# Second-layer evictions given out behind each product, high parts read first, and the PSUM pools swapped

## The chip, the cores and the metric

The kernel runs on one core of one Trainium2 chip. The metric is the device time of one execution in microseconds (us), as the median of several runs. Beside the runs there is one profiled execution, whose trace gives every duration below.

## The reference

First a banded attention (4 batches, 8 heads, 768 positions, 64 wide), whose output becomes the 3072 x 512 matrix `x`. Then a mixture of 8 experts, weighted by a Sinkhorn iteration over the gate's logits:

```python
logits = x @ w_gate
P = np.exp(logits - logits.max())
for _ in range(8):
    P /= P.sum(1, keepdims=True) + 1e-09
    P /= P.sum(0, keepdims=True) + 1e-09
    P *= N / E
for e in range(E):
    h = np.maximum(x @ w1[e], 0.0)
    out += P[:, e:e + 1] * (h @ w2[e])
```

N is 3072, `w1` is 512 x 1024 and `w2` 1024 x 512 for each expert. All is float32.

## The kernel before

**Number form.** Every float32 operand is split into a high and a low part, and a product of two operands takes three TensorE matmuls (high x high, high x low, low x high). Block products go by a seven-product scheme, so each layer of a group is seven products m1 to m7 (first layer) and seven products p1 to p7 (second layer). Each product of one group takes six matmuls of 128x128 by 128x512 (first layer: two parts of the contraction; second layer: two banks of output). The code calls the time of six matmuls a slot (`SLOT = 1.36`).

**Tiling.** Tokens go in three passes. The hidden units of all experts are cut into 31 groups. Groups 0 to 3 are done while attention ends, by another routine (`layer1_strassen` and `second`); its last instructions are the y matmuls, whose results VectorE scales by the gate and adds up, and the exchange of the gate's rows (`between`, that is `spill_rows`: copies to `pcol`, two transposes `pr_ps`, copies to `prow`, DMAs). Groups 4 to 29 of the first pass go in thirteen pairs, (4, 5) to (28, 29). Group 30 follows alone, with a transposed second layer (`turned`, tile `o_t`).

**Order within a pair of the first pass** (called gA and gB). It is written out by the program and kept on each engine (class `Ordered`):
1. first layer of gA: seven slots, m3, m2, m1, m6, m5, m4, m7, in banks c, d, a, b, c, d, a;
2. p6, p4 and p2 of the pair before, which are still owed, follow here ("second" with `behind`), six slots;
3. first layer of gB, seven slots, same banks;
4. p3, p7, p5, p1 of both groups, eight slots.

The last pair has instead an "end" stage with all seven products, fourteen slots, whose results are combined by additions on VectorE and GpSimd (`join`, table `JOIN`).

**First layer** (`layer1_held`). ScalarE copies bank c of m3 to t3 (shown as `early<-bank_c`). VectorE subtracts m2's bank from it, adds t3 and m1's bank to t4, adds that to b of m6, scales, and so on. Every operand of the second layer then gets its high part by a ScalarE cast (`p<-bank_c` is p3's high, `p<-bank_b` p7's, `p<-full` and `p<-bank_d` p5's and p1's) and its low part by a VectorE subtraction (`p<-bank_c,p` is p3's low). The parts of p6, p4 and p2 are given out one by one from a generator in the list `tails` (`x<-bank_c`, `x<-bank_a`, `x<-full` for a gA; `p` for a gB).

**Second layer** (`held_second`). Sums of the second layer live in SBUF. p3, p7, p6 and p4 (`SEEDED`) begin from banks that ScalarE fills with the sum so far (`seed`, shown as `c_acc<-early`), and are emptied by ScalarE copies (`early<-c_acc`). The others are added by VectorE. Each product has two banks. The eviction of a product is noted in `filled_banks`, and given out at the start of the next product or behind the next m3.

**Weights.** In the first pass they are also made, by the generator `maker`: raw weights come by DMA, GpSimd makes sums, ScalarE casts the highs (`w<-raw`, `w<-ext`), GpSimd subtracts the lows (`w<-raw,w`), and the parts are stored in DRAM for passes two and three. A count of slots paces it (`clock`, `LEAD`).

**PSUM.** Pool `mps` has four banks (tag h), the first layer's. Pool `cps` has four banks (tag c), the second layer's; it opens where the y matmuls' pools (`yps`, `sps`) were.

## Time and profile before

| what | value |
|---|---|
| median of 3 runs | 2115.75 us (2113.81 to 2117.53) |
| the profiled execution's own time | 2113.67 us |
| span of its trace | 2111.7 us |
| granted TensorE clock, mean | 0.998 |
| TensorE busy | 2064.1 us, 98% |
| VectorE busy | 1441.8 us, 68% |
| ScalarE busy | 843.7 us, 40% |
| GpSimd busy | 1554.4 us, 74% |

PE is TensorE's matmuls, DVE is VectorE, ACT ScalarE, POOL GpSimd, SP SyncE with its DMA queue. Matmuls are pipelined, so two that follow each other start closer together than one lasts: six matmuls last 1.52 us and start 1.36 us after the six before. A busy share is a mean over stages with different limits; what one stage can give is read in that stage.

### The profile page before, as it was taken

Reading aid. Unit: us, or ns where it says so; the run is one execution under the profiler, and the core shown is the slowest. Engines: PE = TensorE matmul, PEld = TensorE weight load, DVE = VectorE, ACT = ScalarE, POOL = GpSimd, SP = SyncE. Lnnn points to the kernel's source line nnn. Section 1 sums busy time; section 2 is a strip of 40 time slices with the busy share of each in tenths; the row PEclk is TensorE's granted clock in tenths of the full one; section 3 lists DMA queues with packets and bytes.
Section 4 is the critical chain, followed back from the end, with each engine's and each line's share of the span. In section 5 each row is a group of like instructions: output and inputs, shape, how many; then the busy total and the mean of one; then the engine's idle time right before and its main releaser. Section 6 shows DMA issues by size and latency. Waiting matters only on the chain.

```text
span 2111.7 us, 30417 instructions
## 1 busy us (share of the span) xinstructions
PE 2064.1 (98%) x10365; PEld 1705.6 (81%) x10365; DVE 1441.8 (68%) x2539; ACT 843.7 (40%) x1772; POOL 1554.4 (74%) x1392
## 2 busy tenths in 40 slices
PE   8999998999999999999999999999999999999998
PEld 6888887777777777778888888888888888888887
DVE  8777787778888888955665566556746665566556
ACT  7777632565665655323222222222132222222221
POOL 6787886777777777757767767677677767767676
PEclk9999999999999999999999999999999999999999
DMA  6777576777767767795555565555956565566553
GB/s 155 206 219 212 171 261 243 265 259 269 268 252 291 259 255 278 289 350 205 203 201 199 193 210 204 198 204 186 387 207 205 193 211 200 183 209 215 189 205 137
DMA packets 229156, 477.48 MB, mean 226 GB/s; under 512 B 107072, under 2 KB 152576, under 8 KB 205696
## 3 DMA queue, kind: packets, MB, share of 16 engines
q1 hardware_dynamic: 228704, 474.40, 65.4%
q8 instruction: 84, 1.38, 0.3%
q0 software_dynamic: 288, 1.05, 0.1%
q14 instruction: 80, 0.66, 0.1%
HBM read 328.75 MB, written 146.64 MB: 225 GB/s over the span
## 4 chain that ended last, share of the span: by engine, by line
PE 74%; DVE 11%; ACT 5%; POOL 5%; issue 3%; DMA 1%; SPq 0%; ACTq 0%; DVEq 0%; POOLq 0%
PE c_acc L126 31%; PE bank_c L126 9%; PE bank_a L126 9%; PE bank_d L126 9%; PE bank_b L126 5%; PE o_t L126 2%; DVE early L70 2%; ACT p L70 2%; DVE full L70 2%; DVE x L70 1%; DVE p L70 1%; DVE bank_b L70 1%; DVE bank_c L70 1%; ACT w L70 1%; PE o_ps L126 1%
## 5 line engine op out<-in xcount | busy, mean ns | idle before, releaser
L126 PE MATMUL c_acc<-p,w 128*128 128x512 f32 x2838 | 682.4, 391 | 20.4 <-ACT early L70 12.0
L126 PEld LDWEIGHTS c_acc<-p,w 128*128 128x128 f32 x2838 | 529.8, 188 | 145.1 <-ACT early L70 22.4
L1635 DVE TENSOR_TENSOR early<-early,c_acc 128x512 f32<-128x512 f32 x308 | 210.8, 688 | 180.5 <-PE c_acc L126 180.5
L70 POOL TENSOR_TENSOR early<-raw,full 128x512 f32<-128x512 f32 x56 | 72.8, 1299 | 287.4 <-DVE raw L793 287.4
L126 PE MATMUL bank_c<-x,w 128*128 128x512 f32 x1068 | 272.4, 391 | 3.2 <-DVE p L70 3.2
L126 PE MATMUL bank_a<-m,w 128*128 128x512 f32 x1068 | 271.5, 389 | 2.0 <-DVE x L70 1.3
L126 PE MATMUL bank_d<-x,w 128*128 128x512 f32 x1068 | 271.5, 389 | 0.0
L70 POOL TENSOR_TENSOR w<-raw,w 128x512 fp32r<-128x512 f32 (+2 forms) x107 | 184.2, 1722 | 108.5 <-ACT w L70 108.5
L796 ACT CAST p<-raw 128x512 fp32r<-128x512 f32 x150 | 93.3, 622 | 417.9 <-DVE raw L793 328.9
L126 PEld LDWEIGHTS bank_c<-x,w 128*128 128x128 f32 x1068 | 201.1, 188 | 45.4 <-DVE p L70 3.6
L126 PEld LDWEIGHTS bank_a<-m,w 128*128 128x128 f32 x1068 | 200.3, 188 | 44.6 <-DVE x L70 1.8
L126 PEld LDWEIGHTS bank_d<-x,w 128*128 128x128 f32 x1068 | 200.7, 188 | 42.1 <-DMA x<-op_m 0.3
L70 POOL TENSOR_TENSOR p<-raw,p 128x512 fp32r<-128x512 f32 x152 | 196.8, 1295 | 3.7 <-ACT p L796 3.4
L126 PE MATMUL c_acc<-x,w 128*128 128x512 f32 x774 | 196.4, 389 | 0.0
L126 PEld LDWEIGHTS c_acc<-x,w 128*128 128x128 f32 x774 | 145.3, 188 | 30.2
L70 POOL TENSOR_TENSOR p<-full,p 128x512 fp32r<-128x512 f32 x120 | 156.2, 1302 | 3.7 <-ACT p L796 3.7
L804 DVE TENSOR_TENSOR early<-early,bank_d 128x512 f32<-128x512 f32 x63 | 43.3, 688 | 149.5 <-PE bank_d L126 147.1
L796 ACT CAST p<-full 128x512 fp32r<-128x512 f32 x121 | 75.4, 623 | 160.7 <-POOL full L70 140.2
L126 PE MATMUL bank_b<-m,w 128*128 128x512 f32 x534 | 135.5, 389 | 0.0
L126 PEld LDWEIGHTS bank_b<-m,w 128*128 128x128 f32 x534 | 100.2, 188 | 20.8
L371 ACT ACTIVATE p_sb<-p_sb,mx 128x256 f32<-128x256 f32 (+1 forms) x188 | 90.9, 488 | 22.6 <-DVE mx L366 22.1
L802 ACT COPY early<-bank_c 128x512 f32<-128x512 f32 x63 | 37.2, 590 | 150.9 <-PE bank_c L126 150.7
(385 smaller groups left out, 3857.5 us busy)
## 6 DMA issues: line engine op xcount, KB each, us to landing
w<-ws SPq DMA_DIRECT2D x124, 1024.0 KB, 4.9
w<-ws SPq DMA_DIRECT2D x122, 768.0 KB, 4.3
ws<-w SPq DMA_DIRECT2D x54, 1024.0 KB, 4.7
ws<-w SPq DMA_DIRECT2D x53, 768.0 KB, 5.7
raw<-in_moe_w_dram SPq DMA_DIRECT2D x54, 512.0 KB, 4.3
x<-p_rows SPq DMA_DIRECT2D x21, 512.0 KB, 4.9
x<-op_m SPq DMA_DIRECT2D x16, 512.0 KB, 10.5
ws<-w SPq DMA_DIRECT2D x4, 1792.0 KB, 8.5
```

Of the source, the lines that this page charges most:

```text
L70: return lambda *args, **kw: self.tc.keep_in_program_order(op(*args, **kw))
L126: return self.tc.keep_in_program_order(self.engine.matmul(*args, **kw))
L371: scalar.activation(out=views[u], in_=views[u], func=AF.Exp, bias=mx[:, u:u + 1], scale=-1.0, accum_out=sm[:, i, j:j + 1])
L796: engine.copy(out=ops[k][:, 0], in_=src)
L802: nc.scalar.copy(out=t3, in_=c)
L804: tt(out=t3, in0=t3, in1=d, op=ALU.subtract)
L1635: nc.vector.tensor_tensor(out=sums[k][q], in0=sums[k][q], in1=bank, op=ALU.add)
```

## The change

- The eviction of a second-layer product is given out directly behind its own last matmul instead of at the start of the next product or behind m3. The low of p6, p4 or p2 that is still owed follows the eviction.
- The three matmuls of a product now read weight low x operand high, then high x high, then weight high x operand low.
- From the second group on, the first layer works in `cps` and the second layer (`second_banks`) in `mps`; the first group (4) stays in `mps`. Passes two and three and `turned` are swapped likewise.
- `prow` and `pcol` move from a pool to `scratch`, a tile "gap" takes their place in the pool, the rows' exchange comes two y products later, and two of the y products use `mps`.
- In the "end" stage p3 and p7 are seeded, so that they are emptied by ScalarE copies; before, all seven were added by VectorE.
- The making of weights: at the start it runs on until block (5, 0, 0), the first high casts are not tied to the program's order, the gate's share is loaded first, the y spills go on the ordered queue; the last group has leads of its own.

```diff
+LAST_LEAD = {(0, 0): 20, (0, 1): 19, (1, 0): 13}
...
-                    y_ps = moe.layer2(t, wts[g], hs[i], yps, "y")
+                    y_ps = moe.layer2(t, wts[g], hs[i], *((mps, "h") if between and i * WT + t in (3, 4) else (yps, "y")))
...
-                    if between and (i, t) == (0, 1):
+                    if between and (i, t) == (0, 3):
                         between()
...
-                prow = hpool.tile([P, 3, P], F32, name="prow")
-                pcol = hpool.tile([P, E, NB, 2, WT], F32, name="pcol")
+                hpool.tile([P, WIDE], F32, name="gap")
+                prow = scratch[:, 2 * WIDE:2 * WIDE + 3 * P].rearrange("p (n c) -> p n c", n=3)
+                pcol = scratch[:, 3 * WIDE:3 * WIDE + E * NB * 2 * WT].rearrange("p (e b i t) -> p e b i t", e=E, b=NB, i=2)
...
+        def second_banks():
+            return [mps.tile([P, WIDE], F32, name="c_acc", tag="h") for _ in range(2)]
...
-                while clock[0] < used_at[b] - LEAD[layer, part][g % 2] and not hurry[0]:
+                while clock[0] < used_at[b] - (LEAD[layer, part][g % 2] if g < NG - 1 else LAST_LEAD[layer, part]) and not hurry[0]:
...
-                    act(out=high, in_=src)
+                    (act if clock[0] else nc.scalar.copy)(out=high, in_=src)
...
-                return moe.layer1_held(ops, lambda i: block(g, 0, i), share, (full[0], full[3], full[4]), ops_of[g], tmp, mps, "h", done)
-
-            return moe.layer1_scaled(ops, lambda i: blocks_of[g, 0, i], share, free if begins else full, ops_of[g], tmp, mps, "h",
+                return moe.layer1_held(ops, lambda i: block(g, 0, i), share, (full[0], full[3], full[4]), ops_of[g], tmp,
+                                       *((mps, "h") if g == PLAIN else (cps, "c")), done)
+
+            return moe.layer1_scaled(ops, lambda i: blocks_of[g, 0, i], share, free if begins else full, ops_of[g], tmp, cps, "c",
...
-                    o_ps = cps.tile([P, DM], F32, name="o_t", tag="c")
+                    o_ps = mps.tile([P, DM], F32, name="o_t", tag="h")
...
-        def evict():
-            for k, banks, copies, ends in filled_banks:
-                for q, bank in enumerate(banks):
...
+        def evict(k, banks, copies, ends):
+            for q, bank in enumerate(banks):
+                if copies:
+                    Ordered(tc, nc.scalar).copy(out=sums[k][q], in_=bank)
+                else:
+                    Ordered(tc, nc.vector).tensor_tensor(out=sums[k][q], in0=sums[k][q], in1=bank, op=ALU.add)
+            if ends:
+                join(JOIN.get(k, ()))
 
         def done(m):
-            if m == "m3":
-                evict()
-                if tails:
-                    next(tails.pop(), None)
+            if m == "m3" and tails:
+                next(tails.pop(), None)
...
-            seeded = () if begins or ends else SEEDED
+            seeded = () if begins else SEEDED[0:2] if ends else SEEDED
             for n, k in enumerate(ks):
-                evict()
-                if n and tails:
-                    next(tails[0], None)
...
-                        for x, (a, b) in enumerate(((0, 1), (1, 0), (0, 0))):
+                        for x, (a, b) in enumerate(((1, 0), (0, 0), (0, 1))):
...
+                    if g == gs[-1]:
+                        evict(k, banks, begins or k in seeded, ends)
+                        if n and tails:
+                            next(tails[0], None)
                     tick()
-                filled_banks.append((k, banks, begins or k in seeded, ends))
...
-                if follows == "second" and gs is not chunks_of[0][0]:
-                    seeds_next.extend(k for k in ks if k in SEEDED)
+                if follows in ("second", "end") and gs is not chunks_of[0][0]:
+                    seeds_next.extend(k for k in ks or SECOND_ORDER[0:2] if k in SEEDED)
...
+        load_share(0, groups[PLAIN][0])
         hurry[0] = True
-        while (PLAIN, 0, 1) not in ready:
+        while (PLAIN + 1, 0, 0) not in ready:
             next(making)
...
-            nc.sync.dma_start(out=y_spill[u][:, t], in_=acc[:, j])
+            queue.dma_start(out=y_spill[u][:, t], in_=acc[:, j])
```

Where the instructions stand. In a steady pair on ScalarE, behind gB's first layer, these rows stand before (p5's and p1's highs, casts of weights, p3's eviction, **p6's high** from bank c, casts of weights, p7's eviction, p4's high):

```order
L70 CAST p_6599<-full4_5673 128x512
L70 CAST p_6601<-bank_d_6519 128x512
L70 CAST w4_6579<-raw1_5682 128x2x2x128
L70 CAST w4_6579<-ext_5683 128x2x256
L70 COPY early_63<-c_acc_6551 128x512
L70 COPY early_63<-c_acc_6552 128x512
L70 CAST p_6639<-bank_c_6518 128x512
L70 CAST w3_6629<-raw1_5682 128x2x2x128
L70 CAST w3_6629<-ext_5683 128x256
L70 COPY early_63<-c_acc_6564 128x512
L70 COPY early_63<-c_acc_6565 128x512
L70 CAST p_6661<-bank_a_6520 128x512
```

And now:

```order
L71 CAST p_6598<-full4_5672 128x512
L71 CAST p_6600<-bank_d_6520 128x512
L71 CAST w4_6578<-raw1_5681 128x2x2x128
L71 CAST w4_6578<-ext_5682 128x2x256
L71 COPY early_63<-c_acc_6550 128x512
L71 COPY early_63<-c_acc_6551 128x512
L71 CAST w3_6628<-raw1_5681 128x2x2x128
L71 CAST w3_6628<-ext_5682 128x256
L71 COPY early_63<-c_acc_6563 128x512
L71 COPY early_63<-c_acc_6564 128x512
L71 CAST p_6656<-bank_c_6519 128x512
L71 CAST w3_6670<-raw2_5673 128x3x256
```

p3's eviction keeps its place behind two casts of weights; p7's now stands ahead of p6's high.

On ScalarE behind group 4's first layer, before (a cast for the weights, the highs of p6, p4 and p2, group 5's t3 copy, a cast):

```order
L70 CAST w4_5761<-raw2_5674 128x4x256
L70 CAST x00_169<-bank_c_5723 128x512
L70 CAST x10_171<-bank_a_5725 128x512
L70 CAST x11_172<-full3_5672 128x512
L70 COPY early_63<-bank_c_5818 128x512
L70 CAST w4_5831<-raw0_5681 128x4x256
```

And now:

```order
L71 CAST x00_169<-bank_c_5731 128x512
L71 CAST x10_171<-bank_a_5733 128x512
L71 CAST x11_172<-full3_5671 128x512
L71 CAST w4_5780<-raw0_5680 128x4x256
L71 COPY early_63<-bank_c_5827 128x512
L71 CAST w4_5856<-raw1_5681 128x2x2x128
```

The t3 copy of group 5 (here `early_63<-bank_c`) now stands behind a cast of weights of its own.

On GpSimd at the end of the first pass, before (joins are line 1709, the rows with `w3` or `w4` and two inputs are the lows of weights; `w4_10165` is group 30's first block):

```order
L1709 TENSOR_TENSOR early_63<-early_63 128x512 x4
L70 TENSOR_TENSOR ext_5683<-raw0_5681 128x256
L70 TENSOR_TENSOR raw0_5681<-raw0_5681 128x2x128
L70 TENSOR_TENSOR w4_10165<-raw0_5681,w4_10165 128x2x2x128
L70 TENSOR_TENSOR w4_10165<-ext_5683,w4_10165 128x2x256
L70 TENSOR_TENSOR w3_10228<-raw0_5681,w3_10228 128x2x2x128
L1709 TENSOR_TENSOR early_63<-early_63 128x512 x2
L70 TENSOR_TENSOR w3_10228<-ext_5683,w3_10228 128x256
L1709 TENSOR_TENSOR early_63<-early_63 128x512 x2
L70 TENSOR_TENSOR w4_10259<-raw1_5682,w4_10259 128x4x256
L1709 TENSOR_TENSOR extra1_5676<-extra1_5676,early_63 128x512
L1709 TENSOR_TENSOR extra2_5677<-extra2_5677,early_63 128x512
```

And now (joins are line 1710, `w4_10172` is group 30's first block):

```order
L1710 TENSOR_TENSOR early_63<-early_63 128x512 x4
L71 TENSOR_TENSOR ext_5682<-raw0_5680 128x256
L1710 TENSOR_TENSOR early_63<-early_63 128x512 x4
L71 TENSOR_TENSOR raw0_5680<-raw0_5680 128x2x128
L71 TENSOR_TENSOR w4_10172<-raw0_5680,w4_10172 128x2x2x128
L71 TENSOR_TENSOR w4_10172<-ext_5682,w4_10172 128x2x256
L1710 TENSOR_TENSOR extra1_5675<-extra1_5675,early_63 128x512
L1710 TENSOR_TENSOR extra2_5676<-extra2_5676,early_63 128x512
L71 TENSOR_TENSOR w3_10220<-raw0_5680,w3_10220 128x2x2x128
L71 TENSOR_TENSOR w3_10220<-ext_5682,w3_10220 128x256
L71 TENSOR_TENSOR w4_10256<-raw1_5681,w4_10256 128x4x256
```

Group 30's lows, which stood behind p5's four additions, now stand behind p4's four as well.

## Rows read from the trace of the kernel before

**Rows 1.** Windows: stretch, its length, busy time (x count) by engine, clock, DMA share, GB/s.

```profile
339.00:391.00 52.00, 44.55 (x187) 35.43 (x186) 39.30 (x62) 22.68 (x45) 33.82 (x33) 0.97 0.69 249
391.00:858.00 467.00, 450.83 (x1948) 362.88 (x1947) 377.88 (x551) 276.75 (x507) 356.85 (x350) 1.00 0.73 267
858.00:955.00 97.00, 90.05 (x397) 71.99 (x396) 67.60 (x91) 25.43 (x45) 61.00 (x47) 0.98 0.89 334
955.00:2111.00 1156.00, 1151.37 (x5117) 953.50 (x5115) 691.22 (x1016) 293.75 (x492) 837.83 (x664) 1.00 0.60 206
...
895.00:925.00 30.00, 26.66 (x121) 20.89 (x121) 14.35 (x22) 3.07 (x5) 12.12 (x10) 0.94 1.05 398
```

**Rows 2.** Waits of PE, 300 to 950 us: total, times, longest.

```profile
PE c_acc L126 <- ACT early L70: 12.0, 20, 1.0
```

**Rows 3.** Timeline of PE, one steady pair: start, duration, operation [idle before <- releaser].

```profile
447.59 1.52 PE L126 MATMUL bank_c<-x,w 128*128 128x512 f32 x6
...
457.11 1.52 PE L126 MATMUL c_acc<-p,w 128*128 128x512 f32 x6
459.04 4.34 PE L126 MATMUL c_acc<-p,w 128*128 128x512 f32 x18 [0.41 <-ACT p L70]
463.54 3.02 PE L126 MATMUL c_acc<-p,w 128*128 128x512 f32 x12 [0.16 <-ACT early L70]
467.46 3.02 PE L126 MATMUL c_acc<-p,w 128*128 128x512 f32 x12 [0.91 <-ACT early L70]
...
488.00 1.52 PE L126 MATMUL bank_c<-x,w 128*128 128x512 f32 x6
```

**Rows 4.** Timeline of DVE in the same pair.

```profile
450.67 2.15 DVE L70 TENSOR_TENSOR x<-full,x 128x512 fp32r<-128x512 f32 x1
452.75 0.68 DVE L70 TENSOR_TENSOR early<-early,bank_d 128x512 f32<-128x512 f32 x1
...
454.32 0.70 DVE L70 TENSOR_TENSOR bank_b<-bank_b,early 128x512 f32<-128x512 f32 x1
...
458.21 0.68 DVE L70 TENSOR_TENSOR p<-bank_c,p 128x512 fp32r<-128x512 f32 x1
```

**Rows 5.** Timeline of ACT in the same pair.

```profile
462.90 1.07 ACT L70 COPY early<-c_acc 128x512 f32<-128x512 f32 x2
465.51 0.59 ACT L70 CAST p<-bank_c 128x512 fp32r<-128x512 f32 x1 [1.54 <-DVE bank_a L70]
...
466.82 1.07 ACT L70 COPY early<-c_acc 128x512 f32<-128x512 f32 x2
```

**Rows 6.** Timeline of POOL in the same pair.

```profile
449.86 2.40 POOL L70 TENSOR_TENSOR w<-raw,w 128x1024 fp32r<-128x1024 f32 x1 [1.14 <-ACT w L70]
```

**Rows 7.** Timeline of PE, 340 to 392 us.

```profile
343.84 0.33 PE L1311 MATMUL pr_ps<-ident,pcol 128*128 128x128 f32 x1 [1.63 <-ACT pcol L1306]
...
364.35 2.93 PE L126 MATMUL bank_c<-x,w 128*128 128x512 f32 x6 [3.17 <-DVE p L70]
...
370.21 1.65 PE L126 MATMUL bank_a<-m,w 128*128 128x512 f32 x6 [1.32 <-DVE x L70]
...
386.58 3.01 PE L126 MATMUL c_acc<-p,w 128*128 128x512 f32 x12 [0.96 <-ACT early L70]
```

**Rows 8.** Timeline of ACT, 341 to 372 us.

```profile
370.33 0.60 ACT L70 COPY early<-bank_c 128x512 f32<-128x512 f32 x1
```

**Rows 9.** Timeline of PE, 861 to 925 us.

```profile
870.58 5.72 PE L126 MATMUL c_acc<-p,w 128*128 128x512 f32 x24 [2.87 <-DVE early L70]
...
898.91 0.50 PE L126 MATMUL o_t<-w,p 128*128 128x512 f32 x1 [2.64 <-POOL p L70]
...
923.21 1.43 PE L126 MATMUL bank_a<-m,w 128*128 128x512 f32 x5 [0.70 <-DMA m<-op_m]
```

**Rows 10.** Timeline of POOL, 864 to 900 us.

```profile
874.19 5.49 POOL L1709 TENSOR_TENSOR early<-early 128x512 f32<-128x512 f32 x4 [4.46 <-DVE early L70]
...
881.48 1.75 POOL L70 TENSOR_TENSOR w<-raw,w 128x512 fp32r<-128x512 f32 x1
```

More of the change, by code (lines that the diff above doesn't have):

```diff
@@ L1616, in product @@
                 if m == 0:
-                    banks[k] = [cps.tile([P, WIDE], F32, name="c_acc", tag="c") for _ in range(2)]
+                    banks[k] = second_banks()
                 w, h = blocks_of[g, 1, n], ops_of[g][k]
@@ L1639, in second_layer @@
                     next(rest, None)
-        banks_of, filled_banks, tails, seeds_next = {}, [], [], []
+        banks_of, tails, seeds_next = {}, [], []
         def seed(k):
-            banks_of[k] = [cps.tile([P, WIDE], F32, name="c_acc", tag="c") for _ in range(2)]
+            banks_of[k] = second_banks()
             for q, bank in enumerate(banks_of[k]):
                 Ordered(tc, nc.scalar).copy(out=bank, in_=sums[k][q])
-        def evict():
-            for k, banks, copies, ends in filled_banks:
-                for q, bank in enumerate(banks):
-                    if copies:
-                        Ordered(tc, nc.scalar).copy(out=sums[k][q], in_=bank)
-                    else:
-                        Ordered(tc, nc.vector).tensor_tensor(out=sums[k][q], in0=sums[k][q], in1=bank, op=ALU.add)
-                if ends:
-                    join(JOIN.get(k, ()))
-            filled_banks.clear()
+        def evict(k, banks, copies, ends):
[6 more added lines that the diff above has]
+                join(JOIN.get(k, ()))
         def done(m):
-            if m == "m3":
-                evict()
-                if tails:
-                    next(tails.pop(), None)
+            if m == "m3" and tails:
+                next(tails.pop(), None)
             if m in ("m1", "m6") and seeds_next:
@@ L1669, in held_second @@
             begins = gs is chunks_of[0][0]
-            seeded = () if begins or ends else SEEDED
+            seeded = () if begins else SEEDED[0:2] if ends else SEEDED
             for n, k in enumerate(ks):
-                evict()
-                if n and tails:
-                    next(tails[0], None)
                 if k not in banks_of:
-                    banks_of[k] = [cps.tile([P, WIDE], F32, name="c_acc", tag="c") for _ in range(2)]
+                    banks_of[k] = second_banks()
                 banks = banks_of.pop(k)
@@ L1703, in held @@
                 held_second(x, SECOND_ORDER, True)
-                evict()
         def join(todo, gp=nc.gpsimd):
@@ L1760, in pipeline @@
         clock[1] = 2.0
-        load_share(0, groups[PLAIN][0])
         for j in range(BT):
             u, t = divmod(passes[0] * BT + j, UT)
-            nc.sync.dma_start(out=y_spill[u][:, t], in_=acc[:, j])
+            queue.dma_start(out=y_spill[u][:, t], in_=acc[:, j])
         for n, (what, p, x, y) in enumerate(todo):
```

## The prediction

> **What bounds the kernel now.** I read the table by stretches first [rows 1]: in each line the first pair of numbers is the stretch's length and TensorE's busy time in it. From 955 us on TensorE has work in 1151.37 of 1156.00 us, so passes two and three have almost nothing to give, and swapping their PSUM pools changes nothing there that could show. What can be won lies ahead of that: 7.45 idle us between 339 and 391 (the change of stages), 16.17 between 391 and 858 (the eleven pairs of groups of the first pass), 6.95 between 858 and 955 (its end). Next the list of what TensorE waited for [rows 2]: its largest entry is 12.0 us in 20 waits for ScalarE's copies that empty second-layer banks. Then the timeline of one pair on TensorE [rows 3]: in each row the start, the duration, the number of matmuls and, in brackets, the idle time ahead. Six matmuls (a slot) start 1.36 us after the six before them when nothing waits.
>
> The pair runs from 447.59 to 488.00, 40.41 us. It holds 28 slots, 38.08 us. The loss is 2.33 us: 0.57 ahead of 459.04 (459.04 - 457.11 - 1.36), 0.42 ahead of 463.54, 1.20 ahead of 467.46, 0.14 in what follows. An idle of 0.16 in brackets costs 0.42 between starts, so a restart takes some 0.27 beside the idle time.
>
> **The steady pairs.** The three stalls belong to the block p3, p7, p5, p1 behind the pair's second group.
>
> *p3 (0.57).* The group's matmuls on p3's operand must wait for its low part, which VectorE makes last: 458.21 + 0.68 = 458.89 [rows 4], 11.30 after the pair's start. In the old order the low is read by the first of the six (due at 10.88), in the new order by the third (11.33). That alone covers the stall but for some 0.1.
>
> *p5 (0.42).* p5 takes p3's banks, so it waits for the two copies that empty them. ScalarE began them at 462.90, 1.07 for both, the first done at about 463.4 [rows 5]. In the new order these copies keep their place behind p5's and p1's highs and two weight casts; giving the eviction out earlier does not move them. They are early only if the highs are, and these hang on VectorE's chain. There the chain of the second group begins late: the low of p2 took 2.15 us where its neighbours take 0.7, t3 is updated at 452.75, and b at 454.32 [rows 4], although b's product ended at 447.59 + 3 x 1.36 + 1.52 = 453.19. With the evictions of p6 and p4 on ScalarE directly behind their products, p4's high and low lose the wait ahead of them, and b can follow its product at about 453.3: the chain is 1.0 earlier, and p3's eviction too. It then frees its first bank 15.8 - 1.0 = 14.8 after the pair's start; p5 is due at 14.96. Slack 0.1 to 0.2: I count 0.3 of the 0.42.
>
> *p1 (1.20 + 0.14).* Before, p6's high stood ahead of p7's eviction and waited 1.54 for VectorE's last sum, until 465.51, with two casts behind it; the eviction began at 466.82 [rows 5]. Now it stands ahead of p6's high: behind p3's eviction (to 15.4 after the pair's start) and the casts (0.8) its first bank is free at 16.7, p1 is due at 17.7. Slack 1.0: all of it goes. p6's high is later by the eviction's 1.07, and nothing reads it until the next pair's first group is through, seven slots on.
>
> The sum is 0.5 + 0.3 + 1.34 = 2.14 a pair, 23.5 us over eleven. Bounds: all 2.33 (25.6), or p1 alone (14.7).
>
> The low of p2 is the place where a rule speaks against this. The row: 450.67 to 452.82, beside a weight low on GpSimd from 449.86 to 452.26 [rows 6]; VectorE's instruction ended 0.56 behind GpSimd's, just its own working time. The Trainium skill ("SBUF — State Buffer", section Who interferes with whom) says that a VectorE instruction with two SBUF inputs and a GpSimd instruction that reads SBUF lock each other out for the whole instruction; the trace agrees here. By that rule p2's low stays late as long as it meets that cast, and VectorE's chain with it; this is the second case below. I take the chain as free, because the weight's high cast, behind which GpSimd's low waits, now stands ahead of p4's high, so both move forward.
>
> **The change of stages (339 to 391).** The gate's transposes now have six y matmuls behind c_ps ahead of them, which fills 1.36 of a wait of 1.63 plus restarts [rows 7]. It gains nothing at the end of the stretch: VectorE still has its y updates to make, and group 4's chain starts when these end. Group 5 no longer waits for group 4's bank (3.17 at 364.35, then 2.93 for a slot of 1.52, half of TensorE's 2.4 GHz, and 1.32 at 370.21 [rows 7]): its first four products go into the other pool at once. But its fifth takes the bank of its first, which the t3 copy must empty; ScalarE has it behind group 4's x highs and now also a weight cast. It ran at 370.33 to 370.93 [rows 8]; I take 371 to 372. TensorE then stands about 6 us instead of 3.17 + 1.32 and restarts at half clock likewise (1.6: 0.03 of 52 us in [rows 1]). Before, the fifth product began two slots and a bit behind 370.21, at 373.1; now at 371.5 plus 1.6: 0.2 gained within 1.5 either way. The stall at 386.58 (0.96 and a restart, p7's eviction behind p6's high as in the pairs) goes: 1.2. Together **1.4** (0 to 3). The weights' casts ahead of the gate's copies have had nothing else on ScalarE there, and the y spills only change their place on the DMA queue: nothing counted.
>
> **The end (858 to 955).** The wait of 2.87 at 870.58 for VectorE's additions of p3 and p7 [rows 9] goes, since seeded banks are copied by ScalarE; the short wait ahead of it goes as in the pairs. But GpSimd now has the four additions of p4 (1.37 each by 5.49 for four) **ahead** of group 30's first weight lows (1.75), not behind [rows 10]. Without stalls p6 begins at 870.58 - 3.1 - 0.6 + 4 x 1.36 = 872.3, its eviction and VectorE's join are done near 876.5 to 877, GpSimd's four joins near 881.8, a sum (0.7) and the lows near 884.3. Group 30 would be due ten slots behind p5, at 880.5. It waits about **3.9**, and a stall of this size has been followed by half clock (1.6). In return the wait of 2.64 at 898.91 for a low behind the last joins [rows 9] goes, since GpSimd is through by then. Behind 895 the DMA is the limit (share 1.05 [rows 1]), and the operand reload of pass two (0.70 at 923.21 [rows 9]) can land only a little sooner than before. What goes: 2.87 + 2.64 idle, 0.7 in two short waits (6.95 less 2.87, 2.64 and 0.70), 1.1 of restarts, 1.4 of clock, 8.5 to 8.7 in all. What comes: 3.9 + 0.3 + 1.6. Net **2.6**, between -1 (loads decide, nothing else is won) and 4 (no half clock).
>
> **The rivals.** *Main (0.66):* 23.5 + 1.4 + 2.6 = 27.5 off the profiled execution's own 2113.67 gives 2086.2; the median of the runs lies 2.1 above that execution, so **2088.3**. Its own range, 2083 to 2094.
>
> *B, the chain stays late (0.20).* The weight casts remain ahead of p3's eviction and p2's low keeps meeting GpSimd, so p5's stall stays and part of p3's: 0.4 to 1.0 a pair, 5 to 11 us: 2093 to 2099, say 2096. For it: the order of ScalarE's rows there did not change, and a slack of 0.1 is thin. Against: ScalarE is idle between the parts of that chain.
>
> *C, the weights become the bound (0.07).* Each weight block goes through DMA, GpSimd, ScalarE, GpSimd. GpSimd is busy 356.85 of 467 us in the pairs (76%) and would be at 81%. If pairs shrink by only half as planned, 12 us are missing: 2100. Against: TensorE's wait list shows no weight among the larger waits.
>
> *D, the opposite sign (0.04).* The pair's 40.4 us is the pace of the weight chain itself, TensorE's stalls are only where it shows; then the pairs gain nothing, and the late lows of group 30 (3.9 + 1.6) come on top with the 898.91 wait only partly gone: 2118. It decides from the point where that chain needs over 40.2 us a pair. Against: the stalls in [rows 3] have causes of their own in [rows 4, 5].
>
> Left (0.03): the start's stall is much longer than worked out, with a result near 2092 or, with B, above 2100.
>
> **Numbers.** The likeliest is 2088.3. The range reaches from main with all stalls gone and a good end (2082) to B's upper end and C (2100). A run of this kernel tells changes from 0.2% on (4 us): faster 0.95, same 0.02, slower 0.03.
>
> **What the changed kernel's profile would show.** A pair of 38.1 to 38.3 us from one first-group start to the next; p3 and p1 without idle time ahead; a few tenths at most ahead of p5; t3's update at about 4.1 to 4.7 after the pair's start where it was 5.2; an idle stretch of some 6 us in group 5's fifth product, and one of about 4 ahead of group 30's first, waiting for GpSimd's low. Wrong would be: pairs over 39.5 us, a weight as the releaser in the pairs, or no wait ahead of group 30.

## The result, and the profile after

| | before | after |
|---|---|---|
| median | 2115.28 us (4 runs, 2113.81 to 2117.53) | 2089.72 us (4 runs, 2086.84 to 2091.14) |
| ratio | | 0.9877, 95% interval 0.9859 to 0.9894 |
| profiled execution, own time | 2113.67 us | 2091.14 us |

Faster by 25.6 us. The forecast was a median of 2088.3 us, and 27.5 us between the two profiled executions; these lie 22.5 us apart. To see where, I cut both traces at starts of matmuls that both have on TensorE: the last c_ps matmul (a column sum of the Sinkhorn iteration), the first product of group 6, of group 28, and of the second pass.

| stretch, us | before | after | after less before | forecast |
|---|---|---|---|---|
| start of the trace to the last c_ps (after: less 1.36, the y product that now stands ahead of it) | 341.95 | 344.68 | +2.73 | 0 |
| last c_ps to group 6 (before: less the same 1.36) | 46.12 | 46.47 | +0.35 | -1.4 |
| group 6 to group 28, eleven pairs | 444.77 | 421.24 | **-23.53** | **-23.5** |
| group 28 to the second pass | 79.42 | 78.35 | -1.07 | -2.6 |
| second pass to the end of the trace | 1198.1 | 1197.2 | -0.9 | 0 |

The first line is attention and groups 0 to 3, whose matmuls are the same. Over the fourteen profiled executions of this study it lay between 340.8 and 346.6, with no relation to the edits.

The table by stretches of the changed kernel (columns as in [rows 1]) answers to [rows 1]:

```profile
339.00:391.00 52.00, 43.90 (x187) 35.45 (x186) 40.78 (x70) 20.25 (x41) 33.40 (x35) 0.93 0.68 250
391.00:830.00 439.00, 438.74 (x1928) 360.71 (x1927) 363.27 (x545) 273.16 (x504) 353.18 (x346) 1.00 0.78 281
830.00:930.00 100.00, 94.54 (x420) 77.38 (x419) 64.13 (x92) 33.62 (x58) 65.13 (x50) 0.97 0.88 328
930.00:2089.00 1159.00, 1153.86 (x5127) 955.40 (x5126) 692.79 (x1019) 293.85 (x493) 840.28 (x665) 1.00 0.60 206
```

The eleven pairs have 0.26 us of idle TensorE where they had 16.17. What idles now stands at the change of stages (8.1) and at the end (5.5). TensorE's waits from 300 to 950 us (total, times, longest) say the same; the 12.0 us of [rows 2] have become 0.2:

```profile
PE bank_c L127 <- ACT early L71: 7.6, 1, 7.6
PE bank_c L127 <- POOL w L71: 5.0, 1, 5.0
PE bank_a L127 <- DMA m<-op_m: 0.4, 1, 0.4
...
PE c_acc L127 <- ACT early L71: 0.2, 1, 0.2
```

The same pair as in [rows 3], on TensorE (counted, as there, from the first product of its second group):

```profile
448.33 1.52 PE L127 MATMUL bank_c<-x,w 128*128 128x512 f32 x6
...
457.85 11.34 PE L127 MATMUL c_acc<-p,w 128*128 128x512 f32 x48
...
486.71 1.52 PE L127 MATMUL bank_c<-x,w 128*128 128x512 f32 x6
```

It takes 38.38 us instead of 40.41, and p3, p7, p5, p1 run as one block of 48 matmuls. The pairs lie between 38.13 and 38.59, with a mean of 38.29. On VectorE, beside [rows 4]:

```profile
450.60 2.15 DVE L71 TENSOR_TENSOR x<-full,x 128x512 fp32r<-128x512 f32 x1
452.67 0.67 DVE L71 TENSOR_TENSOR early<-early,bank_d 128x512 f32<-128x512 f32 x1
...
454.24 0.70 DVE L71 TENSOR_TENSOR bank_b<-bank_b,early 128x512 f32<-128x512 f32 x1
...
458.13 0.68 DVE L71 TENSOR_TENSOR p<-bank_c,p 128x512 fp32r<-128x512 f32 x1
```

b comes 5.91 after the pair's start (6.73 before), p3's low is ready at 10.48 (11.30). But the low of p2 still takes 2.15. On GpSimd the weight low runs beside it:

```profile
449.79 2.40 POOL L71 TENSOR_TENSOR w<-raw,w 128x1024 fp32r<-128x1024 f32 x1
```

It ends at 452.19, VectorE's instruction 0.56 later, as before [rows 4, 6]. Counted from the pair's start, both only moved forward by the same 0.8. GpSimd's low no longer waits for ScalarE's cast (1.14 in [rows 6]); it now follows GpSimd's own sums directly. On ScalarE, beside [rows 5], p7's eviction is now ahead of p6's high (third row):

```profile
462.81 1.07 ACT L71 COPY early<-c_acc 128x512 f32<-128x512 f32 x2
...
464.60 1.09 ACT L71 COPY early<-c_acc 128x512 f32<-128x512 f32 x2
465.55 0.63 ACT L71 CAST p<-bank_c 128x512 fp32r<-128x512 f32 x1
```

**At the change of stages** TensorE's one long wait is that of group 5's fifth product, for the t3 copy (beside [rows 7]):

```profile
375.57 2.93 PE L127 MATMUL bank_c<-x,w 128*128 128x512 f32 x6 [7.57 <-ACT early L71]
```

Follow it back. On ScalarE the copy stands behind a weight cast, and the cast waits (beside [rows 8]):

```profile
373.99 1.04 ACT L71 CAST w<-raw 128x1024 fp32r<-128x1024 f32 x1 [2.23 <-POOL raw L71]
374.94 0.58 ACT L71 COPY early<-bank_c 128x512 f32<-128x512 f32 x1
```

On GpSimd the sums for that cast wait for the transfer that empties s2, a tile they write again:

```profile
371.42 0.73 POOL L71 TENSOR_TENSOR early<-raw 128x256 f32<-128x256 f32 x1 [8.82 <-DMA s<-early]
```

And on SyncE's queue that transfer stands behind the eight y spills:

```profile
353.64 11.74 SPq L71 DMA_DIRECT2D ys<-early  x8
365.69 0.46 SPq L71 DMA_DIRECT2D s<-early  x1
```

**At the end** TensorE waits for group 30's lows (beside [rows 9]):

```profile
865.40 2.50 PE L127 MATMUL bank_c<-x,w 128*128 128x512 f32 x5 [5.03 <-POOL w L71]
867.71 2.76 PE L127 MATMUL bank_d<-x,w 128*128 128x512 f32 x6
...
901.10 1.45 PE L127 MATMUL bank_a<-m,w 128*128 128x512 f32 x5 [0.43 <-DMA m<-op_m]
```

On GpSimd (beside [rows 10]) p4's four additions and the first low behind them:

```profile
857.11 6.33 POOL L1710 TENSOR_TENSOR early<-early 128x512 f32<-128x512 f32 x4
...
864.08 1.27 POOL L71 TENSOR_TENSOR w<-raw,w 128x512 fp32r<-128x512 f32 x1
```

And TensorE's granted clock (the column 0.50, half of 2.4 GHz) right behind that wait:

```profile
865.40:871.00 5.60, 5.59 (x13) 4.45 (x14) 0.43 (x1) 1.21 (x2) 5.60 (x6) 0.50 0.89 284
```

### The profile page after: what moved, and what is told of

Read it like the earlier page. It is cut to its first block, busy times and chain, and to the rows that moved or that the text cites. A ratio compares the mean times of both kernels' runs of the same rounds, so it can differ in the third digit from the quotient of the medians.

```text
span 2089.3 us, 30417 instructions
## 1 busy us (share of the span) xinstructions
PE 2056.6 (98%) x10365; PEld 1708.5 (82%) x10365; DVE 1422.5 (68%) x2535; ACT 846.8 (41%) x1780; POOL 1556.1 (74%) x1392
## 4 chain that ended last, share of the span: by engine, by line
PE 91%; ACT 3%; DVE 3%; DMA 2%; issue 1%; POOL 0%; SPq 0%; DVEq 0%; ACTq 0%; POOLq 0%
PE c_acc L127 39%; PE bank_c L127 11%; PE bank_a L127 11%; PE bank_d L127 11%; PE bank_b L127 6%; PE o_t L127 2%; ACT p_sb L372 2%; PE o_ps L127 1%; PE s_ps L127 1%; PE y_ps L127 1%; PE t_ps L130 1%; PE h_ps L127 1%; PE tp L130 1%; PE y_ps L993 1%; PE y_ps L994 1%
## 5 line engine op out<-in xcount | busy, mean ns | idle before, releaser
L127 PE MATMUL c_acc<-p,w 128*128 128x512 f32 x2838 | 673.4, 389 | 0.3 <-ACT early L71 0.2
L71 ACT CAST w<-raw 128x512 fp32r<-128x512 f32 (+2 forms) x103 | 82.7, 803 | 41.4 <-POOL raw L71 41.4
```

The source lines that it names most:

```text
L71: return lambda *args, **kw: self.tc.keep_in_program_order(op(*args, **kw))
L127: return self.tc.keep_in_program_order(self.engine.matmul(*args, **kw))
```

## The experiments

Stretches of each run's profiled execution, cut as above (start: last c_ps to group 6, the first five rows less 1.36; end: group 28 to the second pass), and medians:

| run | start | eleven pairs | end | median, us | ratio to before (95%) |
|---|---|---|---|---|---|
| before | 46.12 | 444.77 | 79.42 | | |
| 1 order only | 47.27 | 445.01 | 78.61 | 2115.24 | 1.0 (0.9989 to 1.001) |
| 2 p3, p7, p5, p1 direct | 45.89 | 435.15 | 81.39 | 2105.01 | 0.994 (0.9925 to 0.9955) |
| 3 p6, p4, p2 direct | 47.22 | 432.86 | 77.14 | 2103.22 | 0.9938 (0.9918 to 0.9958) |
| 4 all evictions direct | 44.86 | 423.13 | 79.02 | 2091.78 | 0.9881 (0.9864 to 0.9897) |
| after | 46.47 | 421.24 | 78.35 | 2089.72 | 0.9877 (0.9859 to 0.9894) |
| 5 no swap | 44.29 | 421.00 | 80.21 | 2089.61 | 0.987 (0.9853 to 0.9886) |
| 6 y spills plain | 44.95 | 421.43 | 78.35 | 2093.38 | 0.9895 (0.9879 to 0.9912) |
| 7 end unseeded | 46.86 | 420.64 | 76.53 | 2088.98 | 0.9877 (0.9858 to 0.9896) |
| 8 joins on VectorE | 47.57 | 421.82 | 78.66 | 2088.55 | 0.987 (0.9853 to 0.9886) |
| 9 start and end | 45.82 | 421.90 | 79.02 | 2090.21 | 0.9891 (0.9874 to 0.9907) |
| 10 no swap and end | 44.86 | 421.23 | 78.87 | 2087.96 | 0.9874 (0.9858 to 0.9891) |
| 11 old order | 47.12 | 421.15 | 79.35 | 2091.24 | 0.9895 (0.9879 to 0.9912) |
| 12 t3 first | 48.17 | 420.06 | 78.77 | 2092.58 | 0.9894 (0.9878 to 0.9911) |

Kernels whose start is the same, but for the order of the matmuls, differ in it by up to 1.2 us (before and 1; after, 7, 8 and 11), and 7 and 9, with the same end, differ in it by 2.5. Runs 2, 3 and 4 move evictions of the first and the last pair too, so their starts and ends are not those of before. The pairs of the changed kernel and of runs 5 to 12 agree within 2 us, so the pairs tell most.

**1. The new order of the matmuls alone,** in the kernel before.

```diff
-                        for x, (a, b) in enumerate(((0, 1), (1, 0), (0, 0))):
+                        for x, (a, b) in enumerate(((1, 0), (0, 0), (0, 1))):
```

> The kernel before with one edit, the new order of the three matmuls. Theory A (the stalls at p3, p5 and p1 hang on one another: p5 can start only when p3's eviction frees its bank, 15.95 us after the pair's start, whatever p3 does): p3's 0.57 goes, p5's 0.42 grows to about 0.9 to 1.0, a pair stays at 40.3 to 40.4 us and the time within 2 us of before. Theory B (the sum of the prediction, in which each stall goes by its own edit): a pair takes 39.85 and the kernel about 6 us less.

TensorE in the pair of [rows 3]:

```profile
457.67 5.83 PE L126 MATMUL c_acc<-p,w 128*128 128x512 f32 x24
464.17 3.02 PE L126 MATMUL c_acc<-p,w 128*128 128x512 f32 x12 [0.67 <-ACT early L70]
468.08 3.06 PE L126 MATMUL c_acc<-p,w 128*128 128x512 f32 x12 [0.90 <-ACT early L70]
```

p3's wait is gone, p5's has grown from 0.42 to 464.17 - 457.67 - 4 x 1.36 = 1.06, counted over both, and the pairs take 40.46 on average (40.43 before). Theory A: p5 starts when p3's eviction frees the bank, and what p3 saves, p5 waits.

**2. Only p3, p7, p5, p1 evicted directly,** in the kernel before.

```diff
+                late = k in SECOND_ORDER[SPLIT:]
-                if n and tails:
+                if late and n and tails:
...
+                    if g == gs[-1]:
+                        filled_banks.append((k, banks, begins or k in seeded, ends))
+                        if not late:
+                            evict()
+                            if n and tails:
+                                next(tails[0], None)
                     tick()
-                filled_banks.append((k, banks, begins or k in seeded, ends))
```

> The kernel before, with only the evictions of p3, p7, p5 and p1 given out directly behind their products; those of p6, p4 and p2 and the order of the matmuls stay. Theory A: p1's 1.20 + 0.14 goes (p7's eviction no longer stands behind p6's high), p3's 0.57 and p5's 0.42 stay, since VectorE's chain begins no earlier: a pair of 39.0 to 39.1, about 2099 us. Theory C (the chain's late start has nothing to do with where evictions stand, all of the gain is p7's eviction): the same here, but then the run with the other three evictions moved gains nothing.

```profile
462.75 10.25 PE L126 MATMUL c_acc<-p,w 128*128 128x512 f32 x42 [0.63 <-ACT p L70]
```

p1's wait is gone, as expected, p3's stays (0.5 to 1.2 over the pairs) and p5's is 0.4 in all, as before. A pair takes 39.56 on average, 0.5 more than forecast: VectorE's chain does not come sooner (b 6.95 after the pair's start). That TensorE, with 1.3 less to wait in the block before, comes to it sooner would fit, but is only argued.

**3. Only p6, p4, p2 evicted directly** (the same diff with `late` and `not late` exchanged).

> The kernel before, with only the evictions of p6, p4 and p2 given out directly behind their products. Theory A: VectorE's b comes about 0.8 earlier in the pair (5.9 after its start instead of 6.7), p3's stall goes and p5's falls to 0.1 or 0.2, p1's stays at 1.3 to 1.5 because p6's high still stands ahead of p7's eviction: a pair of 39.5 to 39.7, about 2106 us. Theory C: no change, a pair of 40.4.

TensorE first, then VectorE's b:

```profile
468.61 3.02 PE L126 MATMUL c_acc<-p,w 128*128 128x512 f32 x12 [0.91 <-ACT early L70]
```

```profile
455.45 0.70 DVE L70 TENSOR_TENSOR bank_b<-bank_b,early 128x512 f32<-128x512 f32 x1 [0.20 <-PE bank_b L126]
```

The pair begins at 449.81, so b stands 5.64 after its start, and now waits for TensorE. p3's and p5's waits are both gone, p1's alone is left, a pair of 39.35. Theory C falls: where these three evictions stand sets VectorE's chain.

**4. All evictions direct,** with the old order, pools, start and end: the edits to `evict`, `done` and `held_second` in the change without its new order of matmuls.

> The kernel before with all evictions given out directly, the old order of the matmuls, the old pools, start and end. Theory A: p3's low is ready 10.5 after the pair's start, before the old order needs it (10.9), so the pairs reach 38.2 to 38.4 without the new order; start and end keep their old stalls but those that come from evictions: about 2091 us. Theory B: p3's stall stays by the matmul order, a pair of 38.8, about 2097.

```profile
458.33 11.24 PE L126 MATMUL c_acc<-p,w 128*128 128x512 f32 x48
```

Nine of eleven pairs take 38.1 to 38.5 us, the first 39.90 and the ninth 39.24: 21.6 of the 23.5 us, as theory A has it. In the two long pairs p3 waits, and the chain is that of p2's low and GpSimd's weight low again. VectorE, then GpSimd, in the first pair:

```profile
412.26 2.55 DVE L70 TENSOR_TENSOR x<-full,x 128x512 fp32r<-128x512 f32 x1
```

```profile
411.86 2.39 POOL L70 TENSOR_TENSOR w<-raw,w 128x1024 fp32r<-128x1024 f32 x1
```

GpSimd's low ended 5.31 us after the first pair's start and 4.73 after the ninth's, but 3.5 to 4.0 in the nine others; p2's low ended 0.55 behind it in all eleven. So p3's low was ready at 11.94 and 11.34, where the old order needs it at 10.88. In the first pair GpSimd's sums had waited 1.19 us for a transfer; what delayed them in the ninth stays open.

**5. The changed kernel with the pools as before.**

```diff
-            return [mps.tile([P, WIDE], F32, name="c_acc", tag="h") for _ in range(2)]
+            return [cps.tile([P, WIDE], F32, name="c_acc", tag="c") for _ in range(2)]
...
-                                       *((mps, "h") if g == PLAIN else (cps, "c")), done)
+                                       mps, "h", done)
```

(`layer1_scaled` and `turned` likewise.)

> The changed kernel with the pools as before (first layer in mps, second in cps). Theory A (the swap lets group 5 start early but the time goes into its fifth product): the pairs stay at 38.2 to 38.4, the waits at group 5 come back as idle 3.2 and 1.3, and group 6 starts within 1 us of the changed kernel, counted from the last c_ps: the time is the same within 2 us. Rival: the swap itself carries part of the pairs' gain: pairs of 38.8 or more, 6 us or more lost.

```profile
365.29 2.93 PE L127 MATMUL bank_c<-x,w 128*128 128x512 f32 x6 [3.58 <-DVE p L71]
```

The pairs are unchanged. Of the old waits ahead of group 5 the first is back (3.58, and half clock), the second is not, and the start is shorter by 2.2 than with the swap, where within 1 was expected. The time is the same: the swap earns nothing.

**6. The changed kernel with the y spills on the plain queue.**

```diff
-            queue.dma_start(out=y_spill[u][:, t], in_=acc[:, j])
+            nc.sync.dma_start(out=y_spill[u][:, t], in_=acc[:, j])
```

> The changed kernel with the eight y spills on SyncE's plain queue as before, not the ordered one. In the changed kernel they were issued from 353.6 to 365.4, ahead of the DMA that empties s2 (365.69, landed 371.29), for which GpSimd's sums waited 8.8 us, for them ScalarE's weight cast, and behind it stands group 5's t3 copy (374.94). Theory: without the order the spills go out sooner, the cast no longer waits, the t3 copy stands at about 371.8 and group 5's stall falls by about 3 us; the kernel gains 2 to 3. Rival (it is the transfers themselves that are late, not their place in the queue): the stall stays at 7.5 and the time is the same.

GpSimd, then ScalarE:

```profile
366.37 0.72 POOL L71 TENSOR_TENSOR early<-raw 128x256 f32<-128x256 f32 x1 [5.67 <-DMA s<-early]
```

```profile
369.03 1.06 ACT L71 CAST w<-raw 128x1024 fp32r<-128x1024 f32 x1
369.98 0.60 ACT L71 COPY early<-bank_c 128x512 f32<-128x512 f32 x1
```

The cast no longer waits, and the copy stands 27.7 after the last c_ps instead of 28.9. That is 1.2 instead of the 3 expected: counted from the last c_ps the s2 transfer is issued 3.6 us sooner (16.1 instead of 19.7), but GpSimd can go on only 1.3 sooner (24.1 instead of 25.4). So both were right in part, the place in the queue and the transfers themselves. The copy gains less than the 2.23 that the cast had waited, because another transfer came later: GpSimd got its raw weights 12.8 after the last c_ps instead of 11.0, and group 4's highs, behind a cast that waited for that, began 1.1 later (25.2 instead of 24.1). The start is 1.5 shorter than that of the changed kernel and shorter than in any of 7, 8 and 11; in the time of the whole kernel it does not show.

**7. The changed kernel without seeds in the end stage.**

```diff
-            seeded = () if begins else SEEDED[0:2] if ends else SEEDED
+            seeded = () if begins else () if ends else SEEDED
...
-                if follows in ("second", "end") and gs is not chunks_of[0][0]:
-                    seeds_next.extend(k for k in ks or SECOND_ORDER[0:2] if k in SEEDED)
+                if follows == "second" and gs is not chunks_of[0][0]:
+                    seeds_next.extend(k for k in ks if k in SEEDED)
```

> The changed kernel without the seeds of p3 and p7 in the end stage. Theory A (the end's stall only moves): the wait of about 2.9 for VectorE's additions at p5 is back, group 30's wait for GpSimd's lows falls from 5.0 to about 2, with less half clock behind it: the time is the same within 1.5 us. Rival (each costs by itself): 3 us slower, group 30's wait stays at 5.

```profile
847.20 5.73 PE L127 MATMUL c_acc<-p,w 128*128 128x512 f32 x24 [2.77 <-DVE early L71]
...
867.79 1.43 PE L127 MATMUL bank_c<-x,w 128*128 128x512 f32 x5 [1.03 <-POOL w L71]
```

The old wait is back and group 30's is all but gone; the time is the same. The end's stall moves, as theory A has it.

**8. p4's four additions on VectorE.**

```diff
             if ends:
-                join(JOIN.get(k, ()))
+                join([(int(k == "p4" or j[0]),) + j[1:] for j in JOIN.get(k, ())])
```

> The changed kernel with the four additions behind p4 in the end stage on VectorE, which is idle then, instead of GpSimd. Theory A: GpSimd's lows for group 30 are there about 6 us sooner, its stall of 5.0 and the half clock behind it (2.2 more) go, but the transfers limit what follows: the wait for the reload of the second pass's m7 grows from 0.4 to 3 or 4, so 3 to 4.5 us are gained. Rival 1 (transfers decide alone): the wait grows by all of it, nothing gained. Rival 2 (no limit behind): 7 us gained.

VectorE, then TensorE:

```profile
855.43 7.27 DVE L1710 TENSOR_TENSOR early<-early 128x512 f32<-128x512 f32 x5
...
863.22 5.11 DVE L1710 TENSOR_TENSOR early<-early 128x512 f32<-128x512 f32 x3
```

```profile
870.78 2.92 PE L127 MATMUL bank_d<-x,w 128*128 128x512 f32 x6 [3.40 <-DVE early L805]
```

None of the three expectations: the time is that of rival 1, but no wait for the reload stands for it. Group 30 starts without its wait, but VectorE's additions take 1.45 and 1.70 us each beside GpSimd's lows, where a subtraction of this size with two SBUF inputs took 0.69 with GpSimd idle (366.17 in the changed kernel), and its first step for group 30 is late: 3.40 us, with half clock behind it. The Trainium skill ("SBUF — State Buffer", Who interferes with whom) has the rule, two SBUF inputs against a GpSimd instruction that reads SBUF; the trace agrees in its direction, with these durations.

**9, 10. Versions put together.** 9: plain queue, no seeds at the end, and group 4's last parts behind group 5's first products:

```diff
+            if m in ("m1", "m6", "m5") and early and clock[0] > 7 * SLOT:
+                next(early[0], None)
...
-                if follows != "first":
-                    tails.append(rest)
-                else:
-                    for _ in rest:
-                        pass
+                (early if follows == "first" else tails).append(rest)
```

> The changed kernel with three edits: plain queue for the y spills, no seeds in the end stage, and group 4's last parts (highs and lows of p6, p4, p2) given out behind group 5's m1, m6 and m5 instead of ahead of group 5. Theory A (at the start ScalarE's row order holds the t3 copy, VectorE has room): the copy goes as soon as group 4's last sum has read t3, some 22 us after the last c_ps; group 5's fifth product waits 1 to 2 us instead of 7.6, at full clock, p3 some 2; from the last c_ps to group 6 41 to 43 us (46.5 in the changed kernel, 45.0 with the plain queue). With 1.8 less at the end (from group 28 to the second pass 76.5 instead of 78.35) the kernel takes about 2083 to 2085. Theory B (VectorE's work of groups 4 and 5 is the bound of the start): the wait moves behind group 5 into p3 and p7, 44.5 to 45 us remain, about 2087.

10: pools as before, plain queue, no seeds at the end.

> The changed kernel with the pools as before, the plain queue for the y spills and no seeds in the end stage. If the gains of the stretches add: 44.0 to 44.5 us from the last c_ps to group 6, pairs of 38.2 to 38.3, 76.5 from group 28 to the second pass: 4 us less than the changed kernel, about 2086. Rival: the reload of the second pass's operands limits the end, and what the start gives is all that is left: 2 us.

Neither is better than the changed kernel by more than the measurement tells. In 9 the t3 copy still stood behind the weight cast, which waited 5.01 us for GpSimd; in both p5 of the end stage came 3.7 us late, not 2.9 as in run 7, and the clock was 0.72 in the six us behind it; the end took 79 us.

**11. The changed kernel with the old order of the matmuls.**

> The changed kernel with the old order of the three matmuls. Theory A (with the evictions moved the low is there in time; the order only covers single pairs where VectorE is later, as in two of eleven pairs of the run with the evictions alone): nine or ten pairs unchanged at 38.1 to 38.4, one or two of 38.8 to 39.9, together 1 to 2 us more. Theory B (the order carries p3's stall in every pair): 0.5 in each, pairs of 38.8, 5.5 us more.

Eleven pairs of 38.12 to 38.58, in sum 421.15 against 421.24. The order is worth nothing once the evictions are moved, not even the 1 to 2 us of theory A. In this run no GpSimd low ended later than 3.96 after a pair's start, so the order had no late pair to cover. Runs 6 and 9, with the new order, have one: in their ninth pair that low ended at 4.61 and 4.57, and the pair took 39.12 and 39.09, with the wait at p5 instead of p3. So, by these single pairs, the order does not save such a pair either.

**12. Run 9's start, with the t3 copy ahead of the cast,** and the changed kernel's end.

```diff
+        if soon:
+            copy(out=t3, in_=c)
         done("m3")
-        copy(out=t3, in_=c)
+        if not soon:
+            copy(out=t3, in_=c)
```

(`soon` for group 5 alone.)

> The changed kernel, its end left as it is, with three edits at the start: plain queue for the y spills, group 4's last parts behind group 5's m1, m6 and m5, and group 5's t3 copy given out ahead of the weight cast that stood before it (in the run with the first two alone the copy still waited behind that cast, which waited 5.0 us for GpSimd's sums and they 6.2 us for the transfer of s2). Theory A (that cast is what held the start): the copy runs when group 4's last sum has read t3, about 22.5 us after the last c_ps instead of 27.1; group 5's fifth product waits 1 to 2 us at full clock; VectorE's chain of group 5 begins 3 us sooner, some 3 us are left ahead of p3; from the last c_ps to group 6 42.5 to 43.5 us where the changed kernel has 46.5: about 2086. Theory B (VectorE is the bound of this stretch): p3 and p7 wait for all that m5 no longer waits, 45 us remain and the time is that of the changed kernel.

TensorE, then its clock behind each of the two waits, then ScalarE, then VectorE:

```profile
370.36 2.46 PE L127 MATMUL bank_c<-x,w 128*128 128x512 f32 x6 [1.93 <-ACT early L71]
...
381.92 12.87 PE L127 MATMUL c_acc<-p,w 128*128 128x512 f32 x42 [3.33 <-ACT p L71]
```

```profile
370.40:374.40 4.00, 4.00 (x11) 3.11 (x12) 2.02 (x4) 1.73 (x3) 3.88 (x4) 0.57 0.48 192
...
382.00:388.00 6.00, 5.96 (x13) 4.19 (x14) 5.85 (x10) 3.49 (x7) 2.07 (x3) 0.50 0.80 332
```

```profile
372.67 1.04 ACT L71 CAST w<-raw 128x1024 fp32r<-128x1024 f32 x1 [2.36 <-POOL raw L71]
```

```profile
374.23 0.69 DVE L71 TENSOR_TENSOR x<-bank_c,x 128x512 fp32r<-128x512 f32 x1 [1.95 <-ACT x L71]
...
377.36 2.58 DVE L71 TENSOR_TENSOR x<-full,x 128x512 fp32r<-128x512 f32 x1
```

The fifth product waits 1.93 instead of 7.57, as theory A has it; then p3 waits 3.33, as theory B has it, and the clock is at half twice. The start is no shorter. The cast held the copy, but behind it VectorE, with the lows of group 4 between its steps for group 5, sets when p3 can go. VectorE was not full, though, as theory B has it: it stood 1.95 us for group 4's x high, which ScalarE now makes behind the same weight cast, and p2's low took 2.58 beside a GpSimd low. So that cast still sits in the chain; a start with these highs ahead of it too was not run.

## Why the prediction was right, point by point

**The median (2088.3 forecast, 2089.72 measured): close in part by luck.** Start and end came out 3.3 us worse than forecast, and the profiled executions lie 5.0 us closer together than forecast. But the profiled execution lay 1.6 below its median before, and 1.4 above it after. Two small sums of the prediction do not come out either: 371.5 plus 1.6 is 373.1, so the start gains 1.2 by its own numbers and not 1.4, and 8.5 to 8.7 less 5.8 at the end is 2.7 to 2.9 and not 2.6.

**The pairs (23.5 forecast, 23.53 measured): right in the sum, wrong in how it was shared out.** The sum holds because it counts nearly the whole loss of 2.33 as gone, whichever edit removes it. The prediction gave 0.5 a pair to the order of the matmuls, 0.3 to an earlier p3 eviction, 1.34 to p7's. Runs 1 and 11 show that the order is worth 0, without the moved evictions and with them. The step that failed is "That alone covers the stall but for some 0.1": it covers p3's, and p5 then waits for the same bank as before (run 1: 1.06 instead of 0.42). Run 3 shows p3's and p5's waits together to be VectorE's late chain (1.08 a pair, 40.43 to 39.35), and run 4 that the evictions alone carry 21.6 us.

**The chain.** Forecast 1.0 earlier, measured 0.82 in the pair shown and 0.94 on average. It was not because p2's low was free of GpSimd: it took 2.15 us as before and ended the same 0.56 behind GpSimd's low. So the row held, and with it the rule that the prediction cites from the Trainium skill ("SBUF — State Buffer", Who interferes with whom), and "I take the chain as free" was wrong; the chain came forward because the cast, and GpSimd's low with it, came forward as the same sentence had it. In all but one of the 154 pairs of the fourteen traces p2's low ended 0.54 to 0.56 us behind the GpSimd low beside it. Rival B's price for that case, 0.4 to 1.0 a pair, did not arise.

**What stays in a pair.** Forecast 0.1 to 0.2 ahead of p5; the pairs' mean lies 0.21 above 38.08. It goes with GpSimd's low: pairs of the changed kernel in which that ended 3.5 to 3.6 us after their start took 38.13 or 38.14, those with 3.7 to 3.9 took 38.26 to 38.59. p7's eviction: slack forecast 1.0, no wait seen.

**The start (-1.4 forecast, +0.35 measured).** The mechanism was right, group 5 starts at once and stands at its fifth product. Its size was not: 7.57 us of idle instead of some 6. Two steps failed. The weight cast was priced at its own 1 us, but it waits for GpSimd, GpSimd for a transfer; and "the y spills only change their place on the DMA queue: nothing counted" left out what is queued behind them (run 6: 1.2 us of the copy's time). What the swap gives there depends on the queue: with the ordered one the start takes 44.3 without the swap (run 5) and 46.5 to 47.6 with it (after, 7, 8, 11), with the plain one 44.9 without (run 10) and 45.0 with it (run 6). Run 12 shows that more was not to be had from the copy alone.

**The end (-2.6 forecast, -1.07 measured).** All three waits that were to go are gone, and the one that was to come came: 5.03 instead of 3.9 (p4's additions took 1.58 each, not 1.37), with half clock worth 2.8 instead of 1.6 (17 matmuls from 865.40 to the next product at 872.02, 6.62 us, which take 3.86 at full clock). The term was short by 2.3 us in sum, of which the other terms gave 0.8 back, and run 7 shows that the end is worth the same with the seeds as without. Run 8 shows why the additions cannot simply go to VectorE.

**The rest.** Passes two and three lose as little as before. Rivals C and D fell: no pair waits for a weight, and the pace of 40.4 us was TensorE's, not the weights'. The edits beside the evictions, all together, give no more than the measurement tells: run 4 is at a ratio of 0.9881 (0.9864 to 0.9897), the changed kernel at 0.9877 (0.9859 to 0.9894). Those to the making of weights and to the rows' exchange were not run by themselves.

## What to carry to other kernels

Where several waits hang on one chain, price the chain's end, not each wait: what is saved at the first comes back at the next until the last event (here the eviction that frees a bank) is earlier. A result should be emptied directly behind the product that makes it, ahead of work for later products on the same in-order engine; that placement alone (run 4) gave 21.6 of the pairs' 23.5 us here, and 24.4 of 25.6 us in the medians. And a small copy behind a cast costs what that cast waits for, back to the DMA queue; look there before pricing an edit of a queue's order at nothing.

## What the runs showed of the hardware that was not expected

TensorE's clock did not follow the length of the wait alone. It was at half, for part or all of the stretch that follows, behind waits of 1.93 (run 12), 2.83 (run 4, p5 of the end stage), 3.40 (run 8) and 7.57 us, and at full behind the 2.77 of run 7 and the 2.87 at 870.58 in the kernel before [rows 9]. Run 4, then before:

```profile
850.80:856.20 5.40, 5.36 (x16) 4.25 (x17) 3.78 (x7) 2.14 (x5) 0.76 (x1) 0.68 0.97 311
```

```profile
870.60:876.00 5.40, 5.40 (x24) 4.49 (x25) 5.40 (x9) 2.08 (x5) 1.81 (x2) 1.00 1.00 329
```

What tells these cases apart stays open.

The other is the price of VectorE's additions beside GpSimd's subtractions, 1.45 to 1.70 us for 0.69, while GpSimd's own took 1.74 for 1.27.
